# Another order of the units of a two-branch attention kernel, from its fourth segment on

## The chip, the cores and the metric

One core of a Trainium2 chip runs the whole program. The metric is the device time of one execution in microseconds (us); runs of the same kernel differ by about one microsecond here. Engines: PE multiplies matrices (PEld is its weight loading), ACT (ScalarE) and DVE (VectorE) do elementwise work and empty PSUM, POOL (GpSimd) does elementwise work in SBUF, SP issues DMAs.

## The reference

The input `x` has 2048 tokens of 512 features. Two branches are computed from it and mixed by a gate for each token.

```python
def _A_ref(x, mem0, Wq, Wk, Wv, Wo, seg_len):        # 32 heads of 128, seg_len 32, 8 memory tokens
    mem = mem0
    for s in range(64):
        h = concatenate([mem, x[:, 32*s:32*(s+1)]])  # 40 tokens
        q, k, v = h @ Wq, h @ Wk, h @ Wv             # each 512 -> 32 x 128
        p = softmax(mask(q @ k.T * 128**-0.5))
        o = (p @ v) @ Wo                             # 4096 -> 512
        mem = o[:, :8]                               # the next segment needs this
        outs.append(o[:, 8:])

def _B_ref(x, wq, wk, wv, wo, beta):                 # 32 heads of 16, 4 blocks of 512 tokens
    for s in range(4):
        a_dot = softmax(q_s @ k_s.T * 16**-0.5 + causal) @ v_s
        a_mem = (phi(q_s) @ M) / (phi(q_s) @ z + 1e-6)
        o_s = g * a_mem + (1 - g) * a_dot            # g = sigmoid(beta)
        M, z = M + phi(k_s).T @ v_s, z + sum(phi(k_s))
    return o @ wo

out = g * _A_ref(x) + (1 - g) * _B_ref(x)            # g = sigmoid(x . gate_w)
```

All is bf16 at the borders. Branch A is a recurrence: segment `s+1` cannot start its projections before the eight memory rows that segment `s` put out. Branch B has no such chain that binds.

## The kernel before, in words

After a start-up part (loads, transposes of `x`, most projections of branch B) the kernel holds all weights of branch A in SBUF and goes through the 64 segments of branch A in a chain. It is written as small *units*. A unit plans one piece of work: a few instructions of one engine, sometimes of two or three. A string, `A_ORDER` (L1079 to L1260), lists all units of the whole chain in one order, written out unit by unit. A loop goes through it:

```python
for u in (DEV.get("order") or A_ORDER).split():      # L1780
    v.swap = u[-1] == "~"
    units[u.rstrip("~")]()
```

Each unit appends its instructions to the lists of their engines; an engine runs its own list strictly in that order, and every dependency becomes a semaphore wait. So the string sets two things: the order on every engine and every DMA queue, and, since PSUM banks are handed out first come first served while the string is read (`Banks.take` L58, `give` L70), which bank each unit writes, and so on whose evacuation it must wait.

A `~` behind a unit puts its evacuation on the other engine:

```python
def evac(eng, dst, src, bks, dres, name):            # L391
    if (eng == "act") != v.swap:
        ... ACT: activation(dst, src, Copy)          # L393
    else:
        ... DVE: tensor_copy(dst, src)               # L395
```

The default sides stand in `A_ENG` (L1263): `E0`, `E2`, `H`, `K0`, `K1`, `Q1` and most `L` units of Q on ACT, `E1`, `E3`, `Q0`, `V0`, `V1` on DVE.

The units of segment `s` (written `s.NAME`), b is 0 or 1 for the two halves of the 32 heads:

- `K0x K0y K1x K1y Q0x Q0y V0x V0y V1x V1y`: half a projection each, 8 matmuls of 512 columns over 32-column tiles of the array, four of them side by side (`tokens`, L1303; matmuls at L1316). `Q1x Q1y`: 16 matmuls of 256 columns. They multiply 32 tokens, eight memory tokens of which came from the segment before (`xTp`). Where the unit ahead used the same tokens, the first matmul keeps its weights (`matmul_kept`, whose matmuls have line L19).
- `k0 k1 q0 q1x q1y v0 v1`: evacuation of these (L393 or L395). `TK0 TK1 TQ0 TQ1x TQ1y`: transposes on DVE (L1335).
- `Z`: mask bias into PSUM (L1585, PE). `S0 S1`: scores (L1599, L1604, PE). `X`: exponential (L1613, ACT). `Y`: mask of the first half (L1617, DVE). `M`: sums over the keys (L1635 and L19, PE). `L`: reciprocal through logarithm and exponential (L1641, L1644, ACT). `N`, `n`: normalisation (L1648, DVE, and L1653, POOL).
- `PV`: values (L1665, L1676, PE; takes four banks). `E0` to `E3`: evacuation of them to `OT_sb`. `W0` to `W3`: output projection, 16 matmuls each (L1406, PE).
- `hm`: the new memory. DVE transposes (L1702), moves (L1703) and adds one half (L1707); POOL adds the other half (L1707). The next segment's projections wait for both.
- `H`: evacuation of the output projection to `WN`, `ws`: its store to DRAM. There is one `WN`, which `O` units use as well. `oL`, `qt`: copies on POOL (L1731, L1754).

Beside them stand units with slack, which fill PE while the chain waits: `Lg.*` ("left": projections of the last eight tokens of each of four segments, 32 tokens together), `Og.*` (their output projection, `O.e` evacuation, `O.s` store), `Tg.*` (rows of branch B times its output weights and the final mix and store of 128 rows: `l` load, `b` matmul L1486, `t` ACT L1506, `a` sum L1473, `f` mix L1518), and branch B's attention: `bS` scores (L942, PE, four banks), `bE` exponential of one of them (L963, ACT, and a causal mask on POOL, L969), `bP` values (L995, PE), `bT` one step of its late work (recall from memory on PE L1048, DVE steps), `pj`, `pp` the last block's projections (L846).

Of the kernel before, what the change touches and what calls it, by code (L numbers as in the profile page):

```python
# [877 lines left out]
class BAttn:  # L878
# [212 lines left out]
    L1.VL1x 3.E3~ 3.E0~ 3.E1 L1.VL1y L1.VL1e~ 3.W0 3.W1 3.E2~ 3.W2 3.oL 3.W3 pp bE 3.hm pj 3.H bS pj pp~ bP bP 4.Q0x~ bT bE 4.Q0y 4.K0x~ 4.K0y~ 4.K1x~ 4.q0  # L1091
    4.k0~ 4.qt bE 4.TQ0 bE 4.K1y~ bE L1.VLt 4.k1 L2.xl 4.TK0 4.Q1x~ 4.Q1y 4.TK1 4.S0~ bP 4.q1x 4.q1y bP bS 4.Z1 4.TQ1y 4.X0 4.V1x 4.Y0 4.M0 4.TQ1x bE 4.V1y
    4.S1 bE 4.v1 4.V0x 4.V0y 4.v0 bE 4.X1 4.L0 4.M1 pj 4.n0 pj 4.L1 4.n1 4.N0 4.N1 pj 4.PV~ 3.ws bE pj bP 4.E0 bP 4.E3~ 4.E1 4.E2 4.W0 pp 4.W1 4.W2 4.W3 4.hm
    bS~ O0.0 O0.1 bE bE 5.Q0x~ 5.K0x~ 5.Q0y~ 4.H~ 5.qt bT 5.K0y pp~ bE 5.q0~ 5.K1x~ 5.K1y bT 5.Q1y 5.k0~ 5.TQ0 5.Q1x~ 5.TK0 bE 5.k1 5.q1y 5.TK1 5.Z1 5.S0
    5.TQ1y 5.q1x 5.V1x~ 5.TQ1x 5.X0 5.V0x 5.S1~ 5.Y0 5.V1y 5.M0 5.X1 5.V0y~ 5.L0 5.M1 5.L1 5.v1 5.v0 L2.KL1x 5.N0 5.n0 5.N1 5.n1 bT O0.2 L2.KL1y 5.PV~ bP 4.oL
    5.E0~ bP L2.KL1e~ 6.qt O0.3 5.E1~ bS~ 5.E2 bE 5.E3 4.ws bE O0.e~ 5.W0 5.W1 O0.s 5.W2 5.W3 L2.KL0x L2.KL0y bE bT bE 5.hm bS~ bP bP 6.Q0x~ L2.KL0e~ 6.K0x bE
    6.K0y~ bE 6.Q1x~ bE 6.Q0y 5.H~ 6.Q1y bE 6.q1x~ bS~ 6.q0~ 6.k0~ bP bP 6.K1x~ 6.K1y~ 6.q1y~ 6.TQ0 6.TK0 bE 6.TQ1y bE 6.V0x~ 6.S0 6.TQ1x 6.V1x bE 6.k1~ 6.TK1
    6.V0y~ 6.X0 6.Y0 bT 6.Z1 bE 5.ws 6.S1 6.M0 6.V1y~ 6.X1 6.M1 5.oL 6.L0 6.n0 bP bP 6.v0 6.L1 6.v1 bS 6.N0 6.n1 6.N1 bE 6.PV bT bE L2.QL1x 6.E0 L2.QL1y~ 6.E3
    6.W0 6.E2~ 6.E1~ bE 6.W1 6.W2 6.W3 bE bP bP bS 6.oL L2.QL0x L2.QL1e~ 6.hm L2.QL0y~ 7.qt bT bE bT bE 7.K0x~ 7.Q1y 6.H 7.K0y bT 7.Q0x 7.k0~ 7.Q0y bE bE
    7.K1x 7.q1y~ 7.K1y bP bP 7.q0~ 7.TQ1y 7.TK0 7.TQ0 bS 7.Q1x~ 6.ws L2.QL0e 7.S0~ 7.k1 bE 7.TK1 7.q1x 7.TQ1x 7.X0 7.V1x~ 7.V1y bE 7.Z1 7.S1 7.V0x 7.Y0 7.M0  # L1100
    7.V0y bE 7.X1 7.M1 7.v1 7.L0 7.v0 7.N0 7.n0 L2.VL0x 7.L1 L2.VL1x L2.VL0y 7.n1 7.N1 7.PV 7.E2~ L2.VL1y bE L2.VL0e~ 7.E1~ 7.E0 bP L2.VL1e 8.qt bP bS 7.W0 bE
    7.E3 7.W1 7.W2 bE bE 7.W3 bE 7.hm 8.Z1 bS~ bP 7.H bP 8.K0x 7.oL 8.K0y bE bE 8.Q0x bE 8.Q0y~ 8.K1x 8.k0~ 8.K1y~ bE 8.TK0 8.q0 8.Q1y~ 8.k1 8.Q1x~ 8.TQ0
    8.q1y 8.TK1 8.TQ1y 8.q1x 8.S0~ 8.X0 L3.xl 8.V1x~ 8.V0x 8.TQ1x L2.VLt 8.S1 8.Y0 8.X1 bP 8.M0 8.V0y~ 8.M1 8.V1y 8.v0 7.ws 8.L0 8.N0 8.L1 9.qt 8.N1 L3.KL1x
    O1.0 8.n0 8.v1~ 8.n1 8.PV 8.E0 bP bT 8.E1 L3.KL1y~ 8.E3~ L3.KL1e 8.W0 8.W1 8.E2 8.W2 8.W3 bS~ O1.1 O1.2 8.hm 9.Z1 bE 8.H~ 9.Q1x bE bE 9.K0x 9.q1x~ 9.Q0x
    9.K0y~ 9.Q0y bE 8.ws bT 9.TQ1x 9.k0~ 9.K1x 9.K1y bP 9.TK0 9.q0~ 9.TQ0 9.Q1y 9.S0 9.k1 9.q1y 9.TK1 9.X0 9.TQ1y 9.V1x 9.V1y 9.Y0 9.S1 9.v1 bP 9.X1 9.M0 9.L0
    8.oL 9.V0x 9.N0 9.M1 9.L1 9.V0y~ O1.3 9.v0~ L3.KL0x 9.n0 9.n1 9.N1 9.PV~ 9.E0 bT 9.E1 L3.KL0y~ O1.e~ O1.s 9.E2 bT 9.W0 9.W1 9.E3~ 9.W2 9.W3 L3.KL0e~ 9.hm
    bT bS L3.QL1x bT L3.QL0x 10.Z1 bE 9.oL 10.Q0x~ 10.Q0y bE 10.K0x~ 9.H 10.K0y 10.K1x 10.q0~ 10.qt 10.K1y 10.TQ0 bE 10.k0 10.Q1x 10.k1 10.Q1y 10.TK0 10.TK1
    10.q1x 10.S0 10.TQ1x 10.q1y 10.V1x~ 10.X0 10.V0x~ bE 10.TQ1y 10.Y0 10.S1~ 10.X1 10.V0y 10.M0 10.V1y~ 10.M1 10.L0 L3.VL0x 10.n0 L3.QL0y 10.L1 10.v0 10.n1
    10.v1 9.ws L3.VL0y L3.VL0e~ 10.N0 10.N1 10.PV L3.QL0e~ 11.qt L3.QL1y~ bP 10.E0 11.Z1 10.W0 10.E3 10.E1~ 10.W1 10.E2 10.W2 10.W3 10.hm bP bS T0.l L3.QL1e~
# [24 lines left out]
    19.X0 17.ws L5.VLt 19.TQ1x 19.V1x~ 19.S1~ 19.X1 19.Y0 20.qt 19.V1y 19.M0 L6.xl 18.H~ 19.V0y 19.M1 19.L0 19.v1 19.v0 19.L1 bS~ 19.n0 bP 19.n1 19.N0 19.N1
# [682 lines left out]
```

## Time and profile before

| | |
|---|---|
| median of 3 runs | 820.69 us (820.22 to 821.27) |
| the profiled execution | 821.0 us |
| its span, first to last instruction | 819.2 us |
| granted PE clock | 1.00 |
| busy PE / DVE / ACT / POOL | 782.4 / 568.0 / 559.0 / 306.3 us |
| matmuls, weight loads | 22,701, 20,963 |

A matmul's row tells when it was started and when its last result was out. Four matmuls of one group run side by side, and the next group starts before the marks of the one ahead end, so the time that a group takes is read from start to start. "x16" is 16 instructions merged in one row. `[0.57 <-ACT OT_sb L393]` says that the engine had been idle for 0.57 us and that the ACT instruction at L393 that writes `OT_sb` ended it. A small stop of PE does not show as idle where it is shorter than the marks' overlap.

### The profile page before, as it was taken

Reading aid. Unit: us, or ns where it says so; the run is one execution under the profiler, and the core shown is the slowest. Engines: PE = TensorE matmul, PEld = TensorE weight load, DVE = VectorE, ACT = ScalarE, POOL = GpSimd, SP = SyncE. Lnnn points to the kernel's source line nnn. Section 1 sums busy time; section 2 is a strip of 40 time slices with the busy share of each in tenths; the row PEclk is TensorE's granted clock in tenths of the full one; section 3 lists DMA queues with packets and bytes.
Section 4 is the critical chain, followed back from the end, with each engine's and each line's share of the span. In section 5 each row is a group of like instructions: output and inputs, shape, how many; then the busy total and the mean of one; then the engine's idle time right before and its main releaser. Section 6 shows DMA issues by size and latency. Waiting matters only on the chain.

```text
span 819.2 us, 48809 instructions
## 1 busy us (share of the span) xinstructions
PE 782.4 (96%) x22701; PEld 448.1 (55%) x20963; DVE 568.0 (69%) x1428; ACT 559.0 (68%) x1348; POOL 306.3 (37%) x790
## 2 busy tenths in 40 slices
PE   9988999999999999999999999999999999999996
PEld 4644555555555655555565555455565555556554
DVE  4546667777678867777667677787757677787655
ACT  5545877867757576776766766776576685787643
POOL 4602443433424334253333434344233342454221
PEclk9999999999999999999999999999999999999999
DMA  8996333122212211212313012121212112020322
GB/s 324 417 375 213 90 97 86 43 51 72 60 49 72 56 58 51 59 42 65 90 24 102 28 51 74 31 57 48 81 59 62 53 58 66 26 74 23 87 86 62
DMA packets 100590, 72.17 MB, mean 88 GB/s; under 512 B 58036, under 2 KB 94492, under 8 KB 98844
## 3 DMA queue, kind: packets, MB, share of 16 engines
q1 hardware_dynamic: 99676, 68.24, 27.1%
q8 instruction: 171, 2.80, 1.5%
q10 hardware_dynamic: 704, 0.80, 0.3%
q14 instruction: 39, 0.32, 0.1%
HBM read 43.43 MB, written 25.58 MB: 84 GB/s over the span
## 4 chain that ended last, share of the span: by engine, by line
PE 78%; DVE 7%; ACT 6%; DMA 4%; POOL 2%; issue 2%; SPq 1%; DVEq 0%; POOLq 0%; ACTq 0%
PE ps L1316 37%; PE ps L1406 16%; PE ps L19 6%; PE ps L1665 3%; PE ps L942 2%; PE ps L995 2%; DMA scr_kqd<-stgk 2%; PE ps L708 2%; POOL PTT L969 2%; PE ps L1486 1%; DVE V_sb L395 1%; PE ps L1599 1%; DMA scr_aTd<-WN 1%; ACT PTT L963 1%; DVE P_sb L1648 1%
## 5 line engine op out<-in xcount | busy, mean ns | idle before, releaser
L963 ACT ACTIVATE PTT<-ps 128x512 bf16<-128x512 f32 x320 | 172.0, 603 | 43.8 <-PE ps L942 38.2
L969 POOL TENSOR_SCALAR_AFFINE_SELECT PTT<-PTT 128x128 bf16<-128x128 bf16 (+2 forms) x320 | 120.4, 376 | 127.2 <-ACT PTT L963 103.0
L1316 PE MATMUL ps<-Wv_sb,xTp 128*32 128x512 bf16 x1928 | 141.5, 383 | 0.0
L1406 PE MATMUL ps<-Wo_sb,OT_sb 128*32 128x256 bf16 x4096 | 124.6, 273 | 6.4 <-ACT OT_sb L393 5.3
L1316 PE MATMUL ps<-Wq_sb,xTp 128*32 128x256 bf16 (+1 forms) x2480 | 125.0, 308 | 2.6 <-ACT WN L393 1.5
L1406 PEld LDWEIGHTS ps<-Wo_sb,OT_sb 128*32 128x32 bf16 x4096 | 104.8, 97 | 26.7 <-ACT OT_sb L393 20.9
L1316 PE MATMUL ps<-Wk_sb,xTp 128*32 128x512 bf16 x1592 | 114.3, 379 | 0.5 <-POOL xTp L1707 0.4
L1653 POOL TENSOR_TENSOR P_sb<-P_sb,R_sb 128x64 bf16<-128x64 bf16 x128 | 49.3, 385 | 156.1 <-ACT R_sb L1644 151.5
L1316 PEld LDWEIGHTS ps<-Wq_sb,xTp 128*32 128x32 bf16 x2480 | 65.8, 97 | 60.9 <-issue 32.8
L393 ACT ACTIVATE QN_sb<-ps 128x256 bf16<-128x256 f32 (+1 forms) x146 | 64.4, 447 | 31.9 <-PE ps L1316 31.4
L393 ACT ACTIVATE OT_sb<-ps 128x320 bf16<-128x320 f32 x163 | 61.4, 439 | 31.4 <-PE ps L1676 30.9
L393 ACT ACTIVATE KN_sb<-ps 128x512 bf16<-128x512 f32 x90 | 53.6, 600 | 35.2 <-PE ps L1316 34.8
L1316 PEld LDWEIGHTS ps<-Wk_sb,xTp 128*32 128x32 bf16 x1592 | 44.2, 97 | 60.3 <-issue 30.1
L395 DVE CAST V_sb<-ps 128x512 bf16<-128x512 f32 x85 | 57.9, 686 | 25.8 <-PE ps L1316 24.1
L1335 DVE STREAM_TRANSPOSE KT_sb<-KN_sb 128x256 f32<-128x256 f32 x128 | 55.9, 437 | 18.7 <-ACT KN_sb L393 15.4
L1707 POOL TENSOR_TENSOR xTp<-tt,tu 64x32 bf16<-64x32 f32 x63 | 16.6, 264 | 138.6 <-DVE tu L1703 137.9
L1702 DVE STREAM_TRANSPOSE tt<-ps 128x256 f32<-128x256 f32 x63 | 28.3, 450 | 55.8 <-PE ps L1406 55.0
L1335 DVE STREAM_TRANSPOSE QT_sb<-QN_sb 128x128 f32<-128x128 f32 (+1 forms) x192 | 62.2, 333 | 6.8 <-ACT QN_sb L393 5.2
L1613 ACT ACTIVATE P_sb<-ps 128x224 bf16<-128x224 f32 x128 | 45.6, 357 | 25.5 <-PE ps L1604 22.8
L395 DVE CAST OT_sb<-ps 128x320 bf16<-128x320 f32 x93 | 42.6, 485 | 25.0 <-PE ps L1676 23.7
L1316 PEld LDWEIGHTS ps<-Wv_sb,xTp 128*32 128x32 bf16 x1928 | 41.3, 100 | 22.0 <-issue 9.8
L19 PE MATMUL ps<-Wq_sb,xTp 128*32 128x256 bf16 (+1 forms) x592 | 49.0, 309 | 0.0
(152 smaller groups left out, 1478.9 us busy)
## 6 DMA issues: line engine op xcount, KB each, us to landing
scr_aTd<-WN SPq DMA_DIRECT2D x63, 128.0 KB, 1.9
AR<-scr_aTd SPq DMA_DIRECT2D x60, 96.0 KB
Wk_sb<-in_A_Wk_dram SPq DMA_DIRECT2D x4, 1024.0 KB, 10.5
Wq_sb<-in_A_Wq_dram SPq DMA_DIRECT2D x4, 1024.0 KB, 14.0
Wv_sb<-in_A_Wv_dram SPq DMA_DIRECT2D x4, 1024.0 KB, 13.7
Wo_sb<-in_A_Wo_dram SPq DMA_DIRECT2D x8, 512.0 KB, 6.5
scr_vld<-VNL SPq DMA_DIRECT2D x16, 256.0 KB, 3.3
VL<-scr_vld SPq DMA_DIRECT2D x64, 64.0 KB
```

The source lines that it names most:

```text
L19: return pe.add_instruction(ins)
L393: P.op("act", lambda a: a.activation(dst, src, ACT.Copy), reads=[v.rbank[k] for k in bks], writes=dres, name=name)
L395: P.op("dve", lambda d: d.tensor_copy(dst, src), reads=[v.rbank[k] for k in bks], writes=dres, name=name)
L963: P.op("act", lambda a: a.activation(pt, v.pb[bk], ACT.Exp, scale=v.SCALE_B), reads=[v.rbank[bk]], writes=[rp], name="be%d_%d" % (n, t))
L969: P.op("gp", lambda g: g.affine_select(mv, mv, [[0, len(cut)], [1, 128]], ALU.is_ge, 0.0, base=0, channel_multiplier=-1), reads=[rp], writ ...
L1316: ins = pe.matmul(pb[bk][q, 0:width], lhs(c), w(c, j), start=flags[0], stop=flags[1])
L1335: P.op("dve", lambda d: d.transpose(to, src), reads=reads, writes=writes, name=name)
L1406: ins = pe.matmul(pb[bk][SEG * j:SEG * (j + 1), 0:256], lhs(h), Wo_sb[:, h, :].rearrange("p (k q c) -> p q k c", q=2, c=64)[:, j % 2], sta ...
L1613: P.op("act", lambda a: a.activation(P_sb[:, b, :], pb[bk][:, 0:So], ACT.Exp, scale=SCALE), reads=[rbank[bk]], writes=[Rs("Pm%d" % b), Rs( ...
L1653: P.op(ENG["n"], lambda d: d.tensor_tensor(left, left, grp04(R_sb[:, b, :]), ALU.mult), reads=[Rs("R0_%d" % b)], writes=[Rs("PL%d" % b)], ...
L1665: ins = pe.matmul(pb[bks[j]][:, o:o + L], V_sb[SEG * j:SEG * (j + 1), b, i * E:(i + 1) * E], P_sb[SEG * j:SEG * (j + 1), b, LW * i:LW * i ...
L1702: P.op("dve", lambda d: d.transpose(v.tt[:, :, :].rearrange("p (k n) t -> p k n t", n=2), src), reads=[rbank[wb["bk"]]], writes=[Rs("tt")] ...
```

## The change

Only the string changes. Its first 337 units, up to `3.W3 pp`, stay; the 4,252 after that are the same units in another order. 275 evacuations go to the other of ACT and DVE, about as many in each direction (of the `E` units 6 more on DVE, of the `q1` halves 10 more on ACT, of `k0` and `k1` 8 more on ACT, of `v` 3 more on ACT, of `O.e` 8 more on DVE). No instruction is added or removed but weight loads where a kept weight is lost: counted in the strings, after the change 1,140 projection matmuls keep their weights, 1,232 before. The diff has 170 lines out and 170 in; here are the same stretches of both, segment 8 and the end:

```diff
-    ... 7.hm 8.Z1 bS~ bP 7.H bP 8.K0x 7.oL 8.K0y bE bE 8.Q0x bE 8.Q0y~ 8.K1x 8.k0~ 8.K1y~ bE 8.TK0 8.q0 8.Q1y~ 8.k1 8.Q1x~ 8.TQ0
-    8.q1y 8.TK1 8.TQ1y 8.q1x 8.S0~ 8.X0 L3.xl 8.V1x~ 8.V0x 8.TQ1x L2.VLt 8.S1 8.Y0 8.X1 bP 8.M0 8.V0y~ 8.M1 8.V1y 8.v0 7.ws 8.L0 8.N0 8.L1 9.qt 8.N1 L3.KL1x
-    O1.0 8.n0 8.v1~ 8.n1 8.PV
+    ... 7.hm 7.H bE bE bE L2.VLt bE 8.K0x 8.K0y 8.k0~ bT 8.TK0 8.qt 8.Q0x 8.Q0y~ 8.q0~ 8.TQ0 8.K1x 8.K1y~ 8.k1 8.TK1 8.Q1x~ 8.q1x 8.TQ1x 8.Q1y~ 8.q1y
+    8.TQ1y 8.S0~ 8.X0 8.Y0 8.Z1 8.V1x~ 8.V1y L3.xl 8.S1 8.v1 8.X1 8.M0 7.ws 8.L0 L3.KL1x 8.n0 8.N0 8.V0x 8.M1 8.L1 8.N1 8.V0y~ 8.v0~ L3.KL0x 8.n1 L3.KL1y~
...
-    ... 63.N0 63.n1 T15.b 63.N1 63.PV~ 63.E0 63.E1 63.E3 63.E2 T15.a 63.W0 63.W1 63.W2 63.W3 T15.t 63.H T15.f
+    ... 63.N0 T15.b T15.t 63.n1 63.N1 63.PV~ 63.E2 63.E1~ 63.E0~ 63.W0 63.W1 63.W2 T15.a T15.f 63.E3~ 63.W3 63.H
```

What is to be seen in it: in the new stretch a projection's evacuation and transpose stand right behind its second half (`8.K0x 8.K0y 8.k0~ bT 8.TK0`), where the old one lists other projections between; `bE` units stand in bunches around `hm`; in the last segment `T15.t`, `T15.a` and `T15.f` come before `63.W3`.

More of the change, by code (lines that the diff above doesn't have):

```diff
@@ L1094 @@
[L1094 to L1101, printed above, removed]
@@ L1106 @@
[L1106 to L1109, printed above, removed]
@@ L1261 @@
+    T15.f 63.E3~ 63.W3 63.H
 """
```

326 lines of the change are left out of this document (169 added, 157 removed).

## The prediction

> **What bounds the kernel now.** I read the page first, then the stretch from the first projection of segment 4 to that of segment 63 in the view of windows, because that is where the two orders differ.
>
> ```profile
> span 819.2 us, 48809 instructions
> PE 782.4 (96%) x22701; PEld 448.1 (55%) x20963; DVE 568.0 (69%) x1428; ACT 559.0 (68%) x1348; POOL 306.3 (37%) x790
> ...
> 114.40:803.60 689.20, 665.24 (x20387) 384.67 (x18774) 497.32 (x1263) 484.17 (x1188) 262.62 (x636) 1.00 0.21 59
> ```
>
> PE is the resource: in these 689.2 us it is marked idle for 24.0, at full clock, while DVE and ACT have about 30% to spare. A new order neither adds nor removes a matmul, so PE's own work stays, and what can change is its stops. A matmul's mark outlasts its turn, so the idle time understates the stops. The starts tell:
>
> ```profile
> 405.30 0.37 PE L1665 MATMUL ps<-P_sb,V_sb 32*128 32x40 bf16 x32
> 405.51 0.26 PE L1676 MATMUL ps<-P_sb,VL 32*128 32x64 bf16 x8
> 405.70 0.62 PE L1316 MATMUL ps<-Wk_sb,xL 128*32 128x512 bf16 x8
> 406.17 0.30 PE L995 MATMUL ps<-PTT,Vj 128*32 128x128 bf16 x8
> 406.34 1.93 PE L1406 MATMUL ps<-Wo_sb,OT_sb 128*32 128x256 bf16 x64
> 408.20 0.40 PE L942 MATMUL ps<-KQj 32*128 32x256 bf16 x12
> 408.32 0.45 DVE L1702 STREAM_TRANSPOSE tt<-ps 128x256 f32<-128x256 f32 x1 [1.08 <-PE ps L1406]
> 409.08 0.25 POOL L1707 TENSOR_TENSOR xTp<-tt,tu 64x32 bf16<-64x32 f32 x1 [2.96 <-DVE tu L1703]
> 409.38 0.62 PE L1316 MATMUL ps<-Wq_sb,xTp 128*32 128x256 bf16 x16
> ```
>
> This is segment 28 into 29: values (`PV`), a left-projection half and a `bP` as filling, the output projections (`W0` to `W3`), filling, the new memory's way over DVE and POOL (`hm`), the next segment's first projection. If I give each unit its usual turn (its start to the next unit's start in the fastest tenth of cases: about 0.43 us for a half projection, 0.44 for a `W` unit, 0.11 for a `bP`), the turns leave 55 us of true stops between segments 4 and 63; the window row above groups their 20,387 matmuls. That 55 us, some 0.9 us a segment, is all that an order can win.
>
> **The change part by part.** Every unit is there once in both orders, so nothing is added. I read the new order as a list and asked, for each wait of PE, how much PE work stands between the instruction that starts the wait's chain and the one that waits (its cover). A stop is what the cover falls short of the chain's length. Chain lengths come from cases with little cover:
>
> ```profile
> 299.15 0.24 PE L1635 MATMUL ps<-P_sb,onesb 128*32 128x160 bf16 x4
> ...
> 300.06 0.68 DVE L1648 TENSOR_TENSOR P_sb<-P_sb,R_sb 128x160 bf16<-128x160 bf16 x2
> ...
> 300.88 0.38 PE L1665 MATMUL ps<-P_sb,V_sb 32*128 32x40 bf16 x32 [0.90 <-DVE P_sb L1648]
> 301.09 0.26 PE L1676 MATMUL ps<-P_sb,VL 32*128 32x64 bf16 x8
> 301.92 1.93 PE L1406 MATMUL ps<-Wo_sb,OT_sb 128*32 128x256 bf16 x64 [0.57 <-ACT OT_sb L393]
> ...
> 414.10 0.23 PE L1604 MATMUL ps<-QT_sb,KTL 128*32 128x64 bf16 x4
> 414.41 0.36 ACT L1613 ACTIVATE P_sb<-ps 128x224 bf16<-128x224 f32 x1 [0.59 <-PE ps L1604]
> 414.82 0.25 PE L1635 MATMUL ps<-P_sb,onesb 128*32 128x160 bf16 x4
> ```
>
> - *Values to output projection.* Segment 19 has no filling: 301.92 − 300.88 = 1.04 us, of which 0.38 are the values themselves, so the chain asks for 0.66 us of cover. Segment 28 above takes the same 1.04 us, with 0.54 of useful work in it. Summed over segments 4 to 62, the shortfall is 11.8 us in the old order and 13.2 in the new (eight segments with almost nothing there, against seven): **+1.4 us**.
> - *Last output projection to the next segment.* In segment 28, `W3`'s turn ends at 406.34 + 4 × 0.44 = 408.10; the first projection follows 1.28 us later, with about 1.0 us of filling in it. With 1.2 us asked for (longer fillings end without a stop from there on), the shortfall goes from 4.7 to 3.9: **−0.8 us**.
> - *Second sums to values.* In segment 19 the sums' turn ends at 299.25 and `PV` starts at 300.88; I take 1.33 us as the middle of such cases. The V evacuation asks for less, 0.88 us after the last V half:
>
> ```profile
> L395 DVE CAST V_sb<-ps 128x512 bf16<-128x512 f32 x85 | 57.9, 686 | 25.8 <-PE ps L1316 24.1
> L393 ACT ACTIVATE V_sb<-ps 128x512 bf16<-128x512 f32 x43 | 24.9, 582 | 0.3 <-PE ps L1316 0.2
> ```
>
>  With the larger shortfall of the two taken for each segment, 9.1 us becomes 7.4: **−1.7 us**.
> - *Scores to sums.* From 414.13 (end of the scores' turn) to 414.82 are 0.69 us; with 0.65 for the second half the shortfall goes from 1.8 to 3.2, and for the first half (mask on DVE included, 1.1 us) from 2.4 to 2.8: **+1.8 us**.
> - *Side-attention scores to its values* (`bS` to `bP`, four ACT exponentials between). Cover under 3.4 us falls short by 8.0 us in all before and 6.0 after; the measured stops there are two thirds of that, so **−1.3 us**.
>
> These covers sum to −0.6 us: as far as PE's own list goes, the orders are equals.
>
> *Kept weights.* The new order lets 23 groups of four matmuls fewer keep the weights of the matmul ahead (L19 marks a kept one). Each then needs its loads:
>
> ```profile
> 409.83 0.39 PE L19 MATMUL ps<-Wk_sb,xTp 128*32 128x512 bf16 x4
> 409.83 0.11 PEld L1316 LDWEIGHTS ps<-Wk_sb,xTp 128*32 128x32 bf16 x4
> 410.04 0.39 PE L1316 MATMUL ps<-Wk_sb,xTp 128*32 128x512 bf16 x4
> 410.26 0.39 PE L19 MATMUL ps<-Wq_sb,xTp 128*32 128x512 bf16 x4
> ```
>
> Groups start 0.21 to 0.22 us apart, kept or loaded; the matmul ahead hides the load. Bounds: 0, or 23 × 0.11 = 2.5 us if all were exposed; I take 0. The Trainium skill ("TensorE: Matmul & The Clock Gate", section "LDWEIGHTS (loading the stationary operand)") prices a load by its columns at P/1.2 ns, an estimated 27 ns for 32 columns, so by it 92 loads in a row would cost 2.5 us and speak against the change. The rows here show them hidden.
>
> *The last segment.* The old order puts the last rows' sum (`T15.f`) behind the last segment's own finish on DVE:
>
> ```profile
> 814.89 0.49 DVE L1715 SCALAR_TENSOR_TENSOR WN<-ps,g_sb,KTL 64x256 f32<-64x256 f32 x1 [0.45 <-PE ps L1406]
> 815.42 0.48 DVE L1715 SCALAR_TENSOR_TENSOR KTL<-ps,g_sb,WN 64x256 bf16<-64x256 f32 x1
> 815.82 0.73 DVE L1518 SCALAR_TENSOR_TENSOR aTg<-aTg,g_sb,KQj 96x512 bf16<-96x512 bf16 x1
> 815.92 0.70 SPq L1719 DMA_DIRECT2D out_dram<-KTL  x1
> ...
> 816.67 0.59 SPq L1520 DMA_DIRECT2D out_dram<-aTg  x1
> ```
>
> The new one runs it ahead of `W3`, beside PE's work. The last store is then issued at 815.92, not 816.67: **−0.7 us**.
>
> *The queues.* The stops that my covers explain (11.8 + 4.7 + 9.1 + 1.8 + 2.4 + 5.2 = 35 us) leave 20 of the 55. Those come from ACT, DVE and POOL working through their lists: a step is late because another stands ahead of it.
>
> ```profile
> L1613 ACT ACTIVATE P_sb<-ps 128x224 bf16<-128x224 f32 x128 | 45.6, 357 | 25.5 <-PE ps L1604 22.8
> ...
> ACT P_sb L1613 <- PE ps L1604: 22.8, 44, 1.2
> DVE P_sb L1648 <- ACT R_sb L1644: 9.4, 31, 0.6
> ...
> 320.60 0.38 ACT L393 ACTIVATE WN<-ps 128x256 f32<-128x256 f32 x1 [1.38 <-DMA scr_aTd<-WN]
> 321.04 0.40 PE L942 MATMUL ps<-KQj 32*128 32x256 bf16 x8 [0.63 <-ACT WN L393]
> ```
>
> Only 44 of the 128 exponentials found ACT waiting for PE's scores; in the others ACT came late. In the list, 73 ACT instructions stand between the first scores and their exponential before, 32 after; between second sums and their logarithm 57 and 28; on DVE between second sums and their normalisation 115 and 65. At the exponential's 0.36 us as the price of one, some 25 us of ACT work leave these stretches. Most of it was hidden, and what moves ahead can delay others. I take a tenth, **−2.5 us**, with bounds of −10 (half of the 20 us gone) and +4 (a fifth more). The 320.60 row is such a case: `O4.e` held ACT 1.38 us behind a store from the single buffer `WN`, and PE stopped 0.63; the new order sets it later, so this one goes. Evacuations that change sides (275, about as many each way) stay within the idle shares above; I cost them at nothing beyond this.
>
> Sum: −0.6 − 0.7 − 2.5 = −3.8 us. The profiled execution took 821.0 us (span 819.2 and 1.8 around it), so 817.2; the median of the runs, 820.7, is 0.3 below it, so **816.9 us**.
>
> **Rivals.**
>
> *The memory's hand-over gets late (slower).* DVE works in order, so what stands between `W3` and `hm` delays the transpose on which the next segment hangs:
>
> ```profile
> DVE tt L1702 <- PE ps L1406: 55.0, 51, 2.6
> ```
>
> DVE waited for PE in 51 of 63 hand-overs, which speaks against it: there DVE has room. But the new order lists 37 DVE instructions there, not 28, by their rows 17.5 us, not 13.1, with over 1.6 us in segments 55 and 56 alone. Where DVE is still busy as `W3` ends, each goes straight into the period. If all 4.4 us do and the other queues gain nothing: 820.7 − 0.6 − 0.7 + 4.4 = 823.8 us. The Trainium skill ("TensorE: Matmul & The Clock Gate", section "Architectural detail: the array is 16× 32×32, not 1× 128×128") calls the queues of ACT and DVE strictly first in, first out; by that rule such a step cannot be overtaken, and the 320.60 row agrees.
>
> *Nothing but cover and tail counts.* ACT and DVE have 30% idle, which speaks for it; the 84 late exponentials speak against. 820.7 − 1.3 = 819.4 us.
>
> *The queues were the main loss.* Half of their 20 us goes: 820.7 − 1.3 − 10 = 809.4 us. For it: the counts above halve almost everywhere. Against: evacuations listed earlier must still wait for PE.
>
> **How the numbers follow.** Forecast 0.46, hand-over late 0.25, cover and tail alone 0.16, queues the main loss 0.13. About 0.2% (1.6 us) is what a measurement of this kernel can tell from no change, so 819.1 to 822.3 is "same". Faster takes the forecast and the large gain, 0.59; same the third case, 0.16; slower the hand-over, 0.25. The range reaches from the large gain to the slow rival, 809.4 to 823.8; gains beyond half of the queues' loss, or several losses together, are the rest.
>
> **What would show it.** Right: PE busy within 2 us of now, fewer kept weights (PEld count up by about 92), unchanged half projections at 0.43, PE idle between the same two segments some 3 us less, ACT waiting for the scores (L1613) more than 44 times, the last store about 0.75 us nearer to `W3`. Wrong: the first projection of a segment more often released by POOL or DVE's hand-over, more stops at the output projections than +1.4 us, or PE's turns themselves longer.

## The result and the profile after

The new order is faster by a quarter of a per cent: a median of 818.45 us over 21 runs against 820.39 over 21 runs of the old order, ratio 0.9974 with a 95% interval of 0.9962 to 0.9986. A second timing gave 0.996 [0.9945, 0.9974]. In time that is 2.1 us (1.1 to 3.1) and 3.3 us (2.1 to 4.5), where 3.8 were forecast. Single runs of the old order spread from 818.74 to 824.25 us here, more than the one microsecond that the three runs ahead of the prediction suggested.

The profiled execution of the first timing ran at a granted clock of 0.56 throughout and took 1287.9 us, so the rows below are from a second profile, of the same order at full clock (run `e1_after`). In its file the string takes three lines less, so lines behind L1260 are lower by three: L1313 for L1316, L1403 for L1406, L1610 for L1613, L1517 for L1520.

The page, and the window from the first projection of segment 4 to that of segment 63:

```profile
span 816.4 us, 48934 instructions
PE 783.0 (96%) x22701; PEld 451.9 (55%) x21055; DVE 570.4 (70%) x1431; ACT 559.7 (69%) x1345; POOL 306.8 (38%) x790
```

```profile
113.90:801.85 687.95, 667.02 (x20417) 388.35 (x18882) 500.69 (x1268) 483.84 (x1183) 264.25 (x637) 1.00 0.22 59
```

PE does the same 22,701 matmuls in the same busy time (782.4 before), and loads weights 92 times more (20,963 before). The 59 periods took 687.95 us, 1.25 less than before. PE's idle time in them, by its marks, fell from 24.0 to 20.9 us (687.95 − 667.02). That is the 3 us less that the prediction named as a sign of being right, but 1.8 of it are longer marks for nearly the same matmuls. One trace does not settle such sizes: that of `e2_tail` below, which has the old order in these segments, needs 688.31 us for them and is idle for 22.6.

The groups of the exponentials, and who waited in the view of waits:

```profile
L1610 ACT ACTIVATE P_sb<-ps 128x224 bf16<-128x224 f32 x128 | 45.6, 358 | 27.4 <-PE ps L1601 23.4 <-PE ps L19 3.4
...
ACT P_sb L1610 <- PE ps L1601: 23.4, 42, 0.8
PEld ps L1632 <- ACT P_sb L1610: 15.5, 45, 0.6
DVE tt L1699 <- PE ps L1403: 55.5, 57, 3.2
DVE P_sb L1645 <- ACT R_sb L1641: 13.8, 38, 1.1
```

The same wait of PE in the trace of before:

```profile
PEld ps L1635 <- ACT P_sb L1613: 14.9, 45, 0.8
```

ACT waited for the scores 42 times (44 before; with the waits that ended at L19, 47 and 48) and PE for the exponentials 45 times (45 before): at the exponentials nothing has changed. The normalisations on DVE waited for their reciprocals 38 times (31 before), so DVE more often gets there ahead of ACT. DVE waited for PE in 57 hand-overs (51 before).

The end of the timeline. The last rows' sum and mix (L1470, L1515) now stand ahead of the last segment's own finish (L1712), whose store (L1716) is the last thing issued:

```profile
810.43 0.68 DVE L1470 TENSOR_TENSOR aTg<-PTT 96x512 bf16<-96x512 f32 x1
810.57 1.96 PE L1403 MATMUL ps<-Wo_sb,OT_sb 128*32 128x256 bf16 x64 [0.63 <-DVE OT_sb L395]
811.21 0.75 DVE L1515 SCALAR_TENSOR_TENSOR aTg<-aTg,g_sb,KQj 96x512 bf16<-96x512 bf16 x1
811.99 0.34 SPq L1517 DMA_DIRECT2D out_dram<-aTg  x1
812.58 0.49 DVE L1712 SCALAR_TENSOR_TENSOR WN<-ps,g_sb,KTL 64x256 f32<-64x256 f32 x1 [0.62 <-PE ps L1403]
813.11 0.48 DVE L1712 SCALAR_TENSOR_TENSOR KTL<-ps,g_sb,WN 64x256 bf16<-64x256 f32 x1
813.61 0.70 SPq L1716 DMA_DIRECT2D out_dram<-KTL  x1
```

The output projections end at 810.57 + 1.96 = 812.53, and the store's issue comes 813.61 − 812.53 = 1.08 us later. Before, their row was this:

```profile
812.84 1.93 PE L1406 MATMUL ps<-Wo_sb,OT_sb 128*32 128x256 bf16 x64 [0.57 <-ACT OT_sb L393]
```

It ended at 814.77, and the last store was issued at 816.67, 1.90 us later.

To see where PE stops, each trace was also read unit by unit: a unit's start to the next one's, less the usual turn of such a pair (its fastest twelfth in three of the traces), added up by where the stop lies, segments 4 to 62. It is worked out from the starts of all matmuls.

```
PE's stops, us         old   new   e5     e6     e12    e11    e10    e3     e9     e8
                                   order  sides  E old  exp    softm  pulled hand   fill
own proj., bP, bS      5.7   5.8    9.9   11.1    5.1   15.5   29.8   62.9    9.3    6.3
scores                 1.4   1.9   15.1   11.3    2.0   20.6   38.7   42.9    5.0    2.1
sums                   5.2   5.7    5.1    4.6    5.0    3.6    3.6   19.4    5.0    4.6
values                13.8  10.7   18.5   21.0   10.9   16.0   42.8   30.9   12.6   14.1
values to W0           9.0  11.3   18.6   14.1   16.5    8.9   12.4   10.1   11.5   12.3
W0 to W3               0.6   0.9   14.3    7.6   13.7    0.6    1.5    0.7    0.9    1.2
W3 to next segment    12.7  11.6   13.7   17.8   11.2   10.1   10.9    9.5   17.3   12.0
all                   48.2  47.8   95.1   87.6   64.4   75.3  139.6  176.5   61.6   52.7
```

Old and new differ by 0.4 us in all, and by up to 3 us in single places. The columns to the right belong to the experiments. Such sums hang on which turn is called usual; the prediction's choice gave 55 us for the old order, this one gives 48.2. Worked out again with other choices, the difference of old and new lies between +0.3 and −2.7 us in all, between −1.5 and −3.5 at the values and between +0.8 and +1.6 from the values to `W0`, and the trace of `e2_tail`, with the old order in these segments, comes out 0.8 to 0.9 us below the old one. So the signs of the larger differences hold, but not their tenths. The experiments' differences of 10 us and more stand well clear of this.

### The profile page after: what moved, and what is told of

The parts are those of the page before. It is cut to its first block, busy times and chain, and to the rows that moved or that the text cites. A ratio compares the mean times of both kernels' runs of the same rounds, so it can differ in the third digit from the quotient of the medians.

```text
span 1286.1 us, 48934 instructions
## 1 busy us (share of the span) xinstructions
PE 1269.3 (99%) x22701; PEld 608.5 (47%) x21055; DVE 586.3 (46%) x1431; ACT 586.5 (46%) x1345; POOL 303.7 (24%) x790
## 4 chain that ended last, share of the span: by engine, by line
PE 98%; ACT 1%; DMA 0%; DVE 0%; issue 0%; ACTq 0%
PE ps L1316 51%; PE ps L1406 19%; PE ps L19 7%; PE ps L708 3%; PE ps L942 3%; PE ps L995 2%; PE ps L1486 2%; PE ps L1665 2%; PE ps L846 1%; PE ps L727 1%; PE ps L1599 1%; PE ps L1635 1%; PE ps L1604 1%; PE ps L1585 1%; PE ps L1048 1%; PE ps L1676 1%
## 5 line engine op out<-in xcount | busy, mean ns | idle before, releaser
L1316 PE MATMUL ps<-Wv_sb,xTp 128*32 128x512 bf16 x1940 | 227.7, 579 | 0.0
L1406 PE MATMUL ps<-Wo_sb,OT_sb 128*32 128x256 bf16 x4096 | 208.4, 386 | 4.6 <-ACT OT_sb L393 3.7
L1316 PE MATMUL ps<-Wq_sb,xTp 128*32 128x256 bf16 (+1 forms) x2492 | 202.2, 457 | 0.0
L1316 PE MATMUL ps<-Wk_sb,xTp 128*32 128x512 bf16 x1640 | 188.4, 582 | 0.0
L1406 PEld LDWEIGHTS ps<-Wo_sb,OT_sb 128*32 128x32 bf16 x4096 | 143.8, 127 | 64.0 <-ACT OT_sb L393 19.4
L1316 PEld LDWEIGHTS ps<-Wq_sb,xTp 128*32 128x32 bf16 x2492 | 91.9, 131 | 123.2 <-issue 107.3
L393 ACT ACTIVATE KN_sb<-ps 128x512 bf16<-128x512 f32 x98 | 58.5, 597 | 135.5 <-PE ps L1316 135.4
L1316 PEld LDWEIGHTS ps<-Wk_sb,xTp 128*32 128x32 bf16 x1640 | 61.1, 132 | 120.7 <-issue 119.0
L1335 DVE STREAM_TRANSPOSE QT_sb<-QN_sb 128x128 f32<-128x128 f32 (+1 forms) x192 | 66.9, 352 | 60.9 <-ACT QN_sb L393 54.0
L1316 PEld LDWEIGHTS ps<-Wv_sb,xTp 128*32 128x32 bf16 x1940 | 56.0, 125 | 60.4 <-issue 55.2
L1613 ACT ACTIVATE P_sb<-ps 128x224 bf16<-128x224 f32 x128 | 45.4, 356 | 75.1 <-PE ps L1604 74.7
L19 PE MATMUL ps<-Wq_sb,xTp 128*32 128x256 bf16 (+1 forms) x580 | 66.2, 438 | 0.0
```

The source lines that it names most:

```text
L19: return pe.add_instruction(ins)
L393: P.op("act", lambda a: a.activation(dst, src, ACT.Copy), reads=[v.rbank[k] for k in bks], writes=dres, name=name)
L1316: ins = pe.matmul(pb[bk][q, 0:width], lhs(c), w(c, j), start=flags[0], stop=flags[1])
L1335: P.op("dve", lambda d: d.transpose(to, src), reads=reads, writes=writes, name=name)
L1406: ins = pe.matmul(pb[bk][SEG * j:SEG * (j + 1), 0:256], lhs(h), Wo_sb[:, h, :].rearrange("p (k q c) -> p q k c", q=2, c=64)[:, j % 2], sta ...
L1613: P.op("act", lambda a: a.activation(P_sb[:, b, :], pb[bk][:, 0:So], ACT.Exp, scale=SCALE), reads=[rbank[bk]], writes=[Rs("Pm%d" % b), Rs( ...
```

## The experiments

All are measured as ratio to the kernel before on the same chip, with its 95% interval. In `e1_after` to `e4_nokeep` the lines behind L1260 are lower by two or three; in the later ones they are those of before. PSUM banks are handed out by the string alone, and neither the side of an evacuation nor the place of an exponential takes or gives one. So `e5_order`, `e6_sides`, `e12_E` and `e11_x` keep every bank of the order that they start from, and what they change is the lists of ACT and DVE alone. The others that move many units also change banks: of the 1,413 that a replay of the string hands out, only 368 stay the same in `e3_pull`, 357 in `e10_soft`, 322 in `e7_nofill` and 500 in `e8_fill`. How much of their loss is due to the banks was not tested.

**The same order once more** (`e1_after`, no edit).

> The new order once more, for a profile at full clock. Theory (less waiting in the queues of ACT, DVE and POOL): a ratio to the old order of 0.995 to 0.9985, PE's idle time between the first projection of segment 4 and that of segment 63 lower by 2 to 4 us, and more than 44 exponentials (L1613) for which ACT waits for PE. Rival (cover and tail alone): PE's idle time the same within 1 us and a gain of 0.7 us that stands wholly behind W3 of the last segment.

818.66 us (816.09 to 819.54), ratio 0.996 [0.9945, 0.9974]; its profile is the one shown above. Of the theory's three signs two came: the ratio, and PE's idle time by marks lower by 3.0 us, which the rival (the same within 1 us) did not have. The third, more than 44 exponentials for which ACT waits, did not come (42).

**The tail alone** (`e2_tail`): the old order, with the end in the sequence of the new one.

```diff
-    T15.b 63.N1 63.PV~ 63.E0 63.E1 63.E3 63.E2 T15.a 63.W0 63.W1 63.W2 63.W3 T15.t 63.H T15.f
+    T15.b T15.t 63.N1 63.PV~ 63.E0 63.E1 63.E3 63.E2 63.W0 63.W1 63.W2 T15.a T15.f 63.W3 63.H
```

> The old order; in the last segment alone T15.t, T15.a and T15.f are put ahead of W3, as in the new order. Both theories: the last store is issued 0.75 us sooner after W3, so 0.999 of the time, at the limit of what the measurement tells. Should it come out equal or slower, the three steps delay the evacuations of the values (E) on ACT and DVE.

Ratio 0.9994 [0.9976, 1.0012]: the times can't tell 0.7 us from nothing. The timeline can:

```profile
812.99 1.93 PE L1404 MATMUL ps<-Wo_sb,OT_sb 128*32 128x256 bf16 x64 [0.90 <-ACT OT_sb L393]
...
814.32 0.75 DVE L1516 SCALAR_TENSOR_TENSOR aTg<-aTg,g_sb,KQj 96x512 bf16<-96x512 bf16 x1
...
816.13 0.69 SPq L1717 DMA_DIRECT2D out_dram<-KTL  x1
```

The projections end at 812.99 + 1.93 = 814.92, and 816.13 − 814.92 = 1.21 us pass from there to the last store, against 1.90 before and 1.08 in the new order. So by the traces the tail is worth 0.7 to 0.8 us, as forecast.

**Evacuations pulled ahead** (`e3_pull`): the old order, PE's list as it was; from segment 4 on, each evacuation of K, Q and V stands right behind its second half (394 moved). Segment 34:

```diff
-    34.K0y 34.k0 34.K1y~ bT 34.Q1x 34.Q1y 34.k1 34.TK0 34.Z1 34.S0 34.V0x 34.q1x 34.TK1
+    34.K0y 34.k0 34.K1y~ 34.k1 bT 34.Q1x 34.q1x 34.Q1y 34.q1y 34.TK0 34.Z1 34.S0 34.V0x 34.TK1
```

> The old order of PE's, with each evacuation of a K, Q or V projection from segment 4 on put right behind its second half, as the new order mostly has it (394 units move, PE's order is unchanged). Theory (queues): these evacuations stood behind other work in the lists of ACT and DVE, so this takes 1 to 4 us off by itself. Rival (cover and tail): within 0.1% of the old order, since PE's order is the same.

957.11 us, ratio 1.1643 [1.1619, 1.1667]: 135 us slower, where the theory expected 1 to 4 us of gain and the rival no difference. The waits:

```profile
PEld ps L1597 <- DVE QT_sb L1333: 44.7, 52, 2.0
PEld ps L1663 <- DVE P_sb L1646: 33.5, 32, 2.5
PEld ps L995 <- POOL PTT L969: 24.7, 29, 1.7
```

PE waits for transposes, normalised weights and the masks behind the side exponentials. An evacuation listed ahead of them waits for its own matmuls at the head of the list, and they stand behind it: ACT's idle time before evacuations of Q that PE ended is 71.5 us here and 31.4 before. This ended the simple reading "listed earlier is better". The mean granted clock of the profiled run is 0.989 (1.00 in both kernels), so an estimated 10 us of the loss at most, 0.011 × 951, are the clock's.

**No kept weights** (`e4_nokeep`): the old order, all projections load their weights.

```diff
-        have = P.held == (key, cs[0])
+        have = False
```

> The old order with no projection matmul keeping its weights: 1,232 weight loads more, 13 times what the change adds. If loads hide behind the matmul ahead: within 0.2% of the old order, half projections still 0.43 us from start to start. If each group's load were exposed (0.11 us for four): 308 groups, 34 us slower.

Ratio 1.0014 [0.9995, 1.0032] with 1,232 loads more (PEld of the page):

```profile
PE 785.8 (95%) x22701; PEld 480.1 (58%) x22195; DVE 567.0 (69%) x1428; ACT 559.2 (68%) x1348; POOL 305.9 (37%) x790
```

PEld's busy time grows by 32 us and the run by at most 0.3% (2.6 us). The 92 loads that the change adds are a thirteenth of these, at most 0.2 us.

**The order without the sides** (`e5_order`) **and the sides without the order** (`e6_sides`). First the new order with every evacuation on its old engine, then the old order with every evacuation on its new engine. Segment 29 of the new order and of `e5_order`:

```diff
-    29.PV~ L8.QL0e~ 28.oL T5.a 29.E0 bP bT bT bT 29.W0 29.E1~ 29.E2 29.W1 29.W2 29.E3~ 29.W3 29.hm
+    29.PV~ L8.QL0e~ 28.oL T5.a 29.E0 bP bT bT bT 29.W0 29.E1 29.E2 29.W1 29.W2 29.E3~ 29.W3 29.hm
```

> The new order of the units, with every evacuation on the side that it had before (none of the 275 changes of engine). Theory 1 (the order makes the gain, the sides nothing, as the prediction costed them): the ratio of the new order again, 0.996 to 0.998, some 818.5 us. Rival (the sides belong to the order, since an evacuation that stands directly behind its half finds the one engine free and the other not): half or all of the gain is lost, ratio 0.999 to 1.004; then the stops before the scores and the values grow by some 2 us over those of the new order.

> The old order of the units, with every evacuation on the side of the new order. Theory 1: no difference, ratio 0.999 to 1.001. Rival (the sides carry a part of the gain by themselves): 0.997 to 0.998. Second rival (the sides fit only the new order): slower, 1.002 to 1.006.

868.91 us, ratio 1.0563 [1.0536, 1.059], and 862.17 us, 1.0486 [1.0464, 1.0507]. Neither half does anything but harm, 46 us and 40 us, far beyond what any of the theories expected (ratios up to 1.006), and together they gain 2 to 3. The weight loads of the output projections and of the scores in `e5_order`:

```profile
L1406 PEld LDWEIGHTS ps<-Wo_sb,OT_sb 128*32 128x32 bf16 x4096 | 103.0, 97 | 47.7 <-ACT OT_sb L393 33.4 <-DVE OT_sb L395 9.8 <-issue 0.4
...
L1599 PEld LDWEIGHTS ps<-QT_sb,KT_sb 128*32 128x32 bf16 x2048 | 28.1, 95 | 35.6 <-DVE QT_sb L1335 19.9 <-DVE KT_sb L1335 8.5 <-POOL QT_sb L1754 2.2
```

In the new order with its own sides the first of them waited 28.0 us:

```profile
L1403 PEld LDWEIGHTS ps<-Wo_sb,OT_sb 128*32 128x32 bf16 x4096 | 104.1, 97 | 28.0 <-ACT OT_sb L393 20.9 <-DVE OT_sb L395 2.4 <-issue 1.4
```

By the table of stops the 47 us spread over the scores (+13), the values (+8), the values' evacuations up to `W3` (+21) and the rest.

**The sides of one kind of unit** (`e12_E`): the new order and the new sides, but E0 to E3 on their old engines (100 units). In segment 29 it is the same edit as above, `29.E1~` to `29.E1`.

> The new order and the new sides, but the evacuations of the values (E0 to E3) on their old sides: 100 units change engine against the new order. In the run of the new order with all old sides the stops from the values to the last output projection were 20.6 us longer than with the new sides, of 47 in all. If these stops belong to the E units alone: +17 to +23 us against the new order, ratio 1.017 to 1.025. Rival (the sides of all units only count together): under 5 us, ratio under 1.003, or over 35 us, above 1.04.

836.0 us, ratio 1.0203 [1.0178, 1.0227], some 19 us above the new order, as expected: the stops from the values to `W3` grow by 18.0 us and no others. Segment 29 in the timeline of the new order:

```profile
416.36 1.09 ACT L393 ACTIVATE OT_sb<-ps 128x320 bf16<-128x320 f32 x3
416.51 1.93 PE L1403 MATMUL ps<-Wo_sb,OT_sb 128*32 128x256 bf16 x64
416.60 0.21 DVE L1034 RECIPROCAL oTt<-oTt 128x16 f32<-128x16 f32 x1
416.85 0.73 DVE L1036 SCALAR_TENSOR_TENSOR adot<-oTt,omgBp 128x256 f32<-128x256 f32 x1
417.69 0.72 DVE L1021 STREAM_TRANSPOSE oTt<-ps 128x512 f32<-128x512 f32 x1
```

and of `e12_E`:

```profile
421.65 0.62 PE L1406 MATMUL ps<-Wo_sb,OT_sb 128*32 128x256 bf16 x16
...
421.99 0.73 DVE L1036 SCALAR_TENSOR_TENSOR adot<-oTt,omgBp 128x256 f32<-128x256 f32 x1
422.83 0.72 DVE L1021 STREAM_TRANSPOSE oTt<-ps 128x512 f32<-128x512 f32 x1
423.47 0.45 DVE L395 CAST OT_sb<-ps 128x320 bf16<-128x320 f32 x1
423.97 1.27 PE L1406 MATMUL ps<-Wo_sb,OT_sb 128*32 128x256 bf16 x40 [1.70 <-DVE OT_sb L395]
```

The new order puts three steps of branch B's late work (`bT`) on DVE just there. With `E1` on ACT, all 64 matmuls run through; with `E1` on DVE it stands behind the three, and PE stops for 1.70 us. The side of an evacuation is right or wrong for what stands on that engine's list at that place.

**The softmax steps pulled ahead** (`e10_soft`), **and the exponentials alone** (`e11_x`). The old order, PE's list unchanged. Segment 34 before, in `e11_x` and in `e10_soft`:

```diff
-    34.S0 34.V0x 34.q1x 34.TK1 34.TQ1x 34.q1y 34.X0 34.V0y 34.TQ1y 34.Y0 34.S1~ bE 34.v0 34.M0 34.V1x 34.X1 bT bT 34.M1 33.oL 34.L0 34.n0 34.L1 34.N0
+    34.S0 34.X0 34.V0x 34.q1x 34.TK1 34.TQ1x 34.q1y 34.V0y 34.TQ1y 34.Y0 34.S1~ 34.X1 bE 34.v0 34.M0 34.V1x bT bT 34.M1 33.oL 34.L0 34.n0 34.L1 34.N0
+    34.S0 34.X0 34.Y0 34.V0x 34.q1x 34.TK1 34.TQ1x 34.q1y 34.V0y 34.TQ1y 34.S1~ 34.X1 bE 34.v0 34.M0 34.L0 34.N0 34.n0 34.V1x bT bT 34.M1 34.L1 34.N1
```

> The old order, PE's own list unchanged; from segment 4 on each softmax step stands directly behind what it depends on: X0 behind S0, Y0 behind X0, X1 behind S1, L behind its M, N and n behind L (497 steps moved ahead, past 5 units each on the mean). Theory of the prediction's queue term (a step is late because foreign work stands ahead of it, and listing it earlier wins a tenth to a half of the 20 us): 810 to 818 us, ratio 0.987 to 0.997, stops before the sums and the values down by 2 to 8 us. Rival (what stood between is needed as soon, mostly the evacuation of the second half of Q and the other half's softmax steps, and now waits behind a step that itself waits for PE): slower, ratio 1.005 to 1.05, with longer stops before the second scores and the values.

> The old order with the exponentials alone moved: X0 directly behind S0 and X1 directly behind S1 (100 moved, past 4 units each on the mean), PE's and DVE's lists unchanged but for what the banks ask. It takes away 93 of ACT's instructions that stand between scores and their exponential, more than the new order does (93 to 56). Queue theory: 93 times 0.36 us at a tenth is -3 us, ratio 0.996, with the stops before the first half's sums down by 2 us. Rival: 54 of the 93 are evacuations of Q's second half, which the second scores need; they get late instead, and the stops before the scores and sums together stay the same or grow, ratio 0.999 to 1.01.

914.14 us, ratio 1.1121 [1.1093, 1.115], and 851.96 us, 1.0348 [1.0321, 1.0375]. This is the direct test of the prediction's price for the queues, and it comes out on the other side: taking away the 93 ACT instructions between scores and exponential costs 29 us, and nothing but ACT's list is changed. Both lie beyond the rivals' ranges too, `e10_soft` by 6% and `e11_x` by 2.5%. Segment 34 in the timeline of before:

```profile
470.20 0.72 ACT L393 ACTIVATE QN_sb<-ps 128x256 bf16<-128x256 f32 x2
...
470.40 0.27 PE L1599 MATMUL ps<-QT_sb,KT_sb 128*32 128x40 bf16 x16
...
470.81 0.35 ACT L1613 ACTIVATE P_sb<-ps 128x224 bf16<-128x224 f32 x1
...
471.42 0.27 PE L1599 MATMUL ps<-QT_sb,KT_sb 128*32 128x40 bf16 x16
```

and of `e11_x`:

```profile
482.19 0.27 PE L1599 MATMUL ps<-QT_sb,KT_sb 128*32 128x40 bf16 x16
...
482.58 0.36 ACT L1613 ACTIVATE P_sb<-ps 128x224 bf16<-128x224 f32 x1 [0.48 <-PE ps L1604]
482.84 0.65 ACT L393 ACTIVATE QN_sb<-ps 128x256 bf16<-128x256 f32 x2
483.25 0.59 DVE L1335 STREAM_TRANSPOSE QT_sb<-QN_sb 128x128 f32<-128x128 f32 x2 [0.67 <-ACT QN_sb L393]
483.89 0.28 PE L1599 MATMUL ps<-QT_sb,KT_sb 128*32 128x40 bf16 x16 [0.51 <-DVE QT_sb L1335]
```

Before, ACT empties the second half of Q (470.20) while PE works at the first scores, and the exponential follows at once. In `e11_x` ACT stands idle for 0.48 us in front of the exponential, Q's second half comes behind it, and the second scores start 1.70 us after the first, not 1.02. The groups say the same for the whole run: the exponentials now wait for PE in 99 of 128 cases (44 before), and the idle time before the scores' weight loads has doubled, most of it ended by Q's transposes. The loads' row before, then the rows of `e11_x`:

```profile
L1599 PEld LDWEIGHTS ps<-QT_sb,KT_sb 128*32 128x32 bf16 x2048 | 29.1, 95 | 22.1 <-DVE QT_sb L1335 14.4 <-DVE KT_sb L1335 2.1 <-POOL QT_sb L1754 1.0
```

```profile
ACT P_sb L1613 <- PE ps L1604: 60.8, 99, 1.3
...
L1599 PEld LDWEIGHTS ps<-QT_sb,KT_sb 128*32 128x32 bf16 x2048 | 27.8, 95 | 42.8 <-DVE QT_sb L1335 35.1 <-DVE KT_sb L1335 2.8 <-POOL QT_sb L1754 1.0
```

So an exponential that does not find ACT waiting for it is in itself no sign of a loss. Here it is the sign of a list in which the work that is needed next stands ahead of the step that must wait. The Trainium skill ("TensorE: Matmul & The Clock Gate", section "Architectural detail: the array is 16× 32×32, not 1× 128×128") calls the queues of ACT and DVE strictly first in, first out. By that rule a waiting exponential holds up ready evacuations, and the 0.48 us above agree.

**No filling between the values and the output projection** (`e7_nofill`): the new order; what stood between `PV` and `W0` but the E units (204 units), and what stood between the `W` units and `hm`, now stands behind `hm`, in the old sequence. Four of the copies of the last rows (`oL`) come so late by this that they read what the next segment wrote. Segment 28:

```diff
-    28.PV~ 28.E0 L8.KL0y~ bP bP 28.E1~ bT 27.ws 28.E2 28.W0 28.W1 28.E3~ 28.W2 28.W3 28.hm
+    28.PV~ 28.E0 28.E1~ 28.E2 28.W0 28.W1 28.E3~ 28.W2 28.W3 28.hm L8.KL0y~ bP bP bT 27.ws
```

> The new order without filling between the values and the first output projection: in segments 4 to 62 all that stood between PV and W0 but the evacuations E (204 units) now stands behind hm. Cover theory: the shortfall there goes from 13.2 us to 59 times 0.66 = 38.9, that is +25.7; the stops from W3 to the next segment, 11.6 us in the profile of the new order, can fall by 4 to 10 us. Sum +16 to +22 us, ratio 1.016 to 1.024. Rival 1 (PE makes filling up elsewhere, only its sum counts): within 0.3% of the new order, ratio 0.994 to 1.0. Rival 2 (as with the evacuation sides, the lists of ACT and DVE fall out of step): over 1.04.

949.71 us, ratio 1.1585 [1.1547, 1.1623], where the covers had 1.016 to 1.024 and the second rival over 1.04. At the place itself the covers were right:

```profile
L1406 PEld LDWEIGHTS ps<-Wo_sb,OT_sb 128*32 128x32 bf16 x4096 | 103.6, 97 | 46.8 <-ACT OT_sb L393 36.0 <-DVE OT_sb L395 8.0 <-issue 0.2
```

By the starts of the matmuls, stops of over 0.1 us released by E evacuations went from 11.9 us in 38 units to 41.6 in 60, that is 0.69 us each against the chain's 0.66 and +29.7 us against +25.7 by the covers. But the filling did no good where it went: the stops from `W3` to the next segment grew from 11.6 to 93.8 us, since `bE`, `bP` and the left evacuations now came in one bunch and waited for each other. The mean granted clock of the profiled run is 0.982, so an estimated 17 us of the loss at most, 0.018 × 947, are the clock's.

```profile
PEld ps L995 <- POOL PTT L969: 34.1, 25, 3.7
PEld ps L942 <- DVE oTt L1021: 13.9, 7, 4.1
```

**Filling moved by the covers** (`e8_fill`): the new order with 28 units of filling elsewhere within their segment. One of them, `O15.0`, stands ahead of the copy `62.oL`, so these rows of its product are old ones. One of the 28:

```diff
-    19.M1 19.L1 19.V0y 19.v0 19.N1 18.ws 19.n1 bS~ bE 19.PV
+    19.M1 19.L1 19.V0y bP 19.v0 19.N1 18.ws 19.n1 bS~ bE 19.PV
```

> The new order with 28 moves of filling (halves of left projections, rows' products, bS, bP) within their segment, chosen by the covers and chain lengths of the prediction (with 1.33 us asked for from W3 to the next segment), from waits with more cover than they need to waits with less; nothing else is touched. The shortfalls by that account go from 44.8 to 40.0 us. Cover theory: 3 to 5 us faster than the new order, ratio to the kernel before 0.990 to 0.994. Rival (each move changes the banks and the partners on ACT and DVE, which weighs more than 0.1 to 0.5 us of cover): slower than the new order, ratio 0.998 to 1.02.

822.84 us, ratio 1.0041 [1.0024, 1.0058]: slower than the new order by 0.7%, where the covers promised 3 to 5 us of gain, about 0.5%. Stops grew by 4.9 us, 3.4 of them at the values. Whether the new banks or the new neighbours on ACT and DVE did it, this run can't tell.

**DVE free for the hand-over** (`e9_hand`): the new order; in 16 segments the units with DVE instructions between the last `W` and `hm` stand behind `hm`. Segment 55:

```diff
-    55.W3 L14.VL1e bE bE bE bE bS bT bT bT 56.Z1 55.hm 55.H
+    55.W3 bE bE bE bE bS bT 56.Z1 55.hm L14.VL1e bT bT 55.H
```

> The new order with DVE free for the hand-over: in 16 segments the units with DVE instructions between the last W and hm (bT steps and left evacuations, 35 DVE instructions, some 16 us) stand behind hm. If the hand-over cost the new order what the slower rival said: up to 4.4 us faster than the new order, ratio 0.990 to 0.995. If DVE has room there (it waited for PE in most hand-overs): no difference, 0.995 to 0.998. If the moved steps are needed soon themselves: slower, 0.999 to 1.01.

831.66 us, ratio 1.0148 [1.0128, 1.0169], about 15 us slower than the new order. DVE waited for PE at 60 hand-overs:

```profile
DVE tt L1702 <- PE ps L1406: 70.6, 60, 3.3
```

It had waited at 57 of them in the new order, so there was next to nothing to win. The expectation that fits is the third (the moved steps are needed soon), at more than its 1.01. The loss lies, by the table, from `W3` to the next segment (+5.7 us), at the scores (+3.1) and at the own projections and the side attention (+3.5). Counted by segment, nearly all of it falls into the 16 changed segments and the ones behind them. Segment 31 in the new order:

```profile
439.20 0.68 DVE L395 CAST LN_sb<-ps 128x512 bf16<-128x512 f32 x1
...
440.75 0.40 PE L942 MATMUL ps<-KQj 32*128 32x256 bf16 x8
440.87 0.45 DVE L1699 STREAM_TRANSPOSE tt<-ps 128x256 f32<-128x256 f32 x1 [0.51 <-PE ps L1403]
```

and in `e9_hand`:

```profile
445.03 0.45 DVE L1702 STREAM_TRANSPOSE tt<-ps 128x256 f32<-128x256 f32 x1 [1.58 <-PE ps L1406]
...
445.85 0.68 DVE L395 CAST LN_sb<-ps 128x512 bf16<-128x512 f32 x1
...
446.58 0.40 PE L942 MATMUL ps<-KQj 32*128 32x256 bf16 x8 [1.60 <-DVE LN_sb L395]
```

In the new order DVE empties the left projection's bank (`LN_sb`) while PE still works at the output projections, and the side attention's scores (L942) follow these at once. In `e9_hand` DVE stands idle for 1.58 us in front of `hm`, the evacuation comes behind it, and PE waits 1.60 us for it.

## Why the prediction was nearly right, and where it was not

*The sign and the size.* Forecast −3.8 us; measured −2.1 (−3.1 to −1.1) in the first timing and −3.3 (−4.5 to −2.1) in the second. The sign was right, and the result lies between the forecast and the case in which only cover and tail count (−1.3). The first timing is nearer to that case, the second to the forecast, so the times do not choose between the two. The traces and `e11_x` speak against the forecast's extra term, the queues.

*Covers, −0.6.* By the table of stops the places moved the way that the covers had them: values to `W0` +2.3 (forecast +1.4), `W3` to the next segment −1.1 (−0.8), at the values −3.1 (−1.7), sums and scores +1.0 (+1.8). The stops at the output projections thus grew by more than 1.4 us, which the prediction had named as a sign of being wrong; with other choices of the usual turn they grew by 0.8 to 1.6 up to `W0`, so it isn't settled. The side attention's values lie in several rows of the table; their stops over 0.1 us went from 3.7 to 2.0 us (forecast −1.3). All stops together fell by 0.4 us, where the covers had −0.6, but both are below what single traces can tell. What a chain asks for was confirmed apart from the sum by `e7_nofill` (0.69 us for 0.66).

*Kept weights, 0.* Right: 92 more loads were counted, and 1,232 more cost at most 2.6 us.

*Tail, −0.7.* Right: the last store comes 0.82 us nearer to the projections' end in the new order and 0.69 us nearer with the tail alone.

*Queues, −2.5.* This is the step that failed, and with it a sign in the list of what would show the forecast right: ACT was to wait for the scores more than 44 times, and it did 42 times. With the covers' −0.6 it asked for 3.1 us less in segments 4 to 62; they took 1.25 us less, and the table has 0.4 us of it as stops. PE's idle time by marks did fall by the forecast 3 us, but marks are what the prediction itself had called misleading. The reasoning took every ACT instruction between scores and exponential for foreign work that delays it. Counted by name, 54 of the 93 were evacuations of Q's second half and 13 of K's, which the second scores need, and of the 98 before the logarithms 86 were softmax steps of the same segment. `e11_x` shows the price of moving the exponential past them: 29 us of loss, not 3 of gain. The new order empties its counts in another way, with most of Q's evacuations ahead of the scores, and what that is worth alone no run shows. That the total came out near the forecast therefore owes something to luck: about 1 us of the first timing's 2.1, and 2 of the second's 3.3, have no shown cause.

*Evacuation sides, nothing beyond the queues.* Right in sum by luck, wrong as reasoning. The idle share of ACT and DVE (30%) says nothing of what a swap costs: the same 275 swaps on the old order cost 40 us, and without them the new order loses 46. Had the diff held one half only, the forecast would have been off by ten times its size.

*The slower rival.* Its place was wrong: DVE had room at the hand-overs (in 57 of 63 it waited for PE), and the first projections waited no more often for the new memory (`xTp` of POOL: 41 times, 45 before). Making more room cost some 15 us.

*What stays open.* Of the 3.0 us between the last instructions on the engines in the two traces, 0.7 lie after the last output projection, 1.2 lie in segments 4 to 62, 0.5 in segment 63 and 0.6 in the part ahead of segment 4. The last says nothing: in five traces with the old order up to there (`before`, `e2_tail`, `e3_pull`, `e10_soft`, `e11_x`) the first projection of segment 4 starts between 114.06 and 115.63 us, and in the new order at 114.21. The 1.2 us in the segments are little more than the 0.9 by which two traces of the old order differ. Which units of the new order bring that gain isn't settled by these runs; only the tail's part has a place.

## What to carry to other kernels

In a written-out order on engines that work strictly through their lists, an instruction that waits blocks everything behind it, so "listed earlier" is no gain by itself: ask of each step what ready work it would stand in front of. Order and evacuation side are one decision; never price one with the other held fixed, and never take a share of idle time for room at one place. Covers price a single wait well (0.69 us for 0.66) but not a rearrangement: 28 moves worth −4.8 us by cover gave +4.9 us of stops.

## What was not expected

- At PE busy 96% of the span these orders stand on a narrow ridge: every edit of the lists tried here but the given one and the tail's cost between 0.7% (28 units) and 16% (394 units), although no work was added.
- Moving 100 exponentials past four units each on the mean cost 29 us, 0.3 us for each, with PE's, DVE's and POOL's lists and all banks as they were.
